# A start-up with x's first tile loaded in two halves and its third tile multiplied within contraction step 1

## The chip, the cores and the metric

The kernel runs on one core of a Trainium2 chip. The metric is the device time of one execution in microseconds (us). Four runs of the kernel before the change took 177.17 to 177.66 us, with a median of 177.25. The core has five engines that matter here: PE (matrix multiply; PEld is its weight load), DVE (vector), ACT (scalar), POOL (GpSimd) and SP (issues most DMAs). ACT can issue DMAs as well.

## What is computed

```python
xn = layernorm(x)                      # x: (2048 tokens, 512), bf16
out = x + SSM(xn) + (gelu(xn @ w_gate) * (xn @ w_up)) @ w_down

def SSM(x):                            # 512 complex states
    dt = exp(log_dt); Lam = Lambda_re + 1j * Lambda_im
    Lam_bar = exp(dt * Lam)
    Bu = x @ (((Lam_bar - 1) / Lam)[:, None] * B).T
    h[t] = Lam_bar * h[t-1] + Bu[t]
    return 2 * (h @ C.T).real + x * Dskip
```

The gate and up weights are 512 x 1376 each, w_down is 1376 x 512.

## The kernel before

The 2048 tokens are cut into 16 tiles of 128 rows, and four tiles make a block; 512 tokens of a block are one matmul's moving width. The contraction over the 512 features takes four steps (k = 0 to 3) of 128. For a block, the kernel normalises x on DVE, transposes it with DMA transposes (TR), multiplies it with w_gate and w_up (GU, L842), with B (BU, L748), runs the recurrence on DVE as a scan between two rotations (CHAIN, L773 to L803), and adds everything up in PSUM (DN, L883) before the output is added to the skip term and stored (L901).

The first block is started in another way, since at its beginning neither the normalised x nor the weights are there. Its tiles are only centred (the row mean is taken off, `sub`, `cent`), transposed by PE against an identity matrix (`cent_T`, L679), and copied from PSUM to the transposed tile XC by ACT or DVE (L686, L688). `GT_k` (L700) then multiplies one tile j by one 128-row step k of the weights, into the PSUM banks 2j and 2j + 1; the division by the standard deviation follows later, as the scale of the gelu (`GT_evac`, L720 and L723). `GT_mm` (L711) does the same for all four steps at once, for tile 3 and for further columns. So PE can start on a weight step as soon as that step has landed.

What sets the order: PE and SP run in program order. On DVE, ACT and POOL a list scheduler sets it, from modelled durations and due times; `order_behind` and `ch(...)` chain some operations by hand, and in the start-up nearly all of DVE's are. The scheduler derives all waits from which buffers overlap.

The names of the start-up: `ld_x0` (L492) loads a tile of x; tiles 0, 2 and 3 go over SP's queue, in front of and between the weight loads (`ld_wk`, L482, for gate and up of each step), tile 1 over ACT's queue, behind the instruction that loads the activation table and after DVE's second memset. Three small parameter loads (L506) follow on ACT's queue. PE begins with seven matmuls on constants (`nwarm`, L925 to L934) and with short ones in between (`fill`). Tile 0's row sum is taken on DVE (L965), tile 1's mean on ACT (L954); both tiles are centred in two pieces, of 128 and 384 columns (`cent`, L957). Tiles 2 and 3 get their mean from the layer norm's statistics on DVE (`stats`, L610 and L611; `sub`, L948). `ks(k, j, ...)` issues the step-k matmuls of tile j. In PE's order tiles 0 and 1 take steps 0 and 1, tile 2 is transposed, tiles 0 and 1 take step 2, and tile 2 then takes steps 0, 1 and 2; step 3 follows for all three, with the transposes of tile 3 behind the first of them.

Of the kernel before, what the change touches and what calls it, by code (L numbers as in the profile page):

```python
# [353 lines left out]
def d_dve_1x(n): return 100.0 + 1.04 * n  # L354
def d_dve_scan(n): return 90.0 + 2.08 * n
def d_dve_ts4x(n): return 220.0 + 0.26 * n
D_TINY = 160.0
def d_act(n, ptr=0): return 190.0 + 0.833 * n + 90.0 * ptr
# [3 lines left out]
def build(nc, ins, out):  # L362
    with ExitStack() as es:
        E = es.enter_context
        S = Sched(nc, es)
# [6 lines left out]
        def ring(parent, name, n):  # L372
            return [A.sub(parent, "%s%d" % (name, i), i) for i in range(n)]
# [14 lines left out]
        X = ring(X_all, "X", NT)  # L388
# [70 lines left out]
        x2 = ins["A_x"][0]  # L459
# [6 lines left out]
        GATE = {"before_gelu": [], "nh": 0}  # L466
        SCR = A.alloc("SCR", [1], F32)
        half = V(lambda e: e.memset(HALF.ap, 0.5), D_TINY, [], [HALF], "half")
        wrm = S.order_behind(V(lambda e: e.memset(WRM.ap, 0.0), 150, [], [WRM], "wrm"), half)
# [21 lines left out]

        def ld_x0(j, queue="sync", after=()):  # L492
            return S.dma(lambda e, j=j: e.dma_start(X[j].ap, x2[128 * j:128 * (j + 1), :]), 128 * 1024, writes=[X[j]], tag="ld_x0", queue=queue, after=after)  # L493
        ld_x0(0)
        GATE["par"] = S.order_behind(ld_x0(1, "scalar", [wrm]), GATE["table"])
        for k in range(KD):
            if k in (1, 3):
                ld_x0((k + 3) // 2)
# [109 lines left out]
        def stats(b, j):  # L608
            tt = 4 * b + j
            return (V(lambda e: e.bn_stats(ST[tt].ap, X[tt].ap), d_dve_1x(512), [X[tt]], [ST[tt]], "bnst"),  # L610
                    V(lambda e: e.bn_aggr(MVt[b][j].ap, ST[tt].ap), D_TINY, [ST[tt]], [MVt[b][j]], "bnag"))  # L611

        def root(b, j0, j1):
            mn, sbq, qb, rq = (cols(t, b, j0, j1) for t in (MN, SBQ, QB, RQ))
            mv = Buf("MV%d_%d_%d" % (b, j0, j1), "sb", MVt[b][j0].lo, MVt[b][j1 - 1].hi, MV[b].ap[:, j0:j1])
            op = V(lambda e: e.tensor_scalar(sbq.ap, mv.ap[:, :, 1], EPS_BF16, None, ALU.add), D_TINY, [mv], [sbq], "sbq")
            GATE["pow"] = POOL(lambda e: e.tensor_tensor(qb.ap, sbq.ap, HALF.ap[:, 0:j1 - j0], ALU.pow), 1100, [sbq, HALF], [qb], "pow")
            POOL(lambda e: e.tensor_copy(mn.ap, mv.ap[:, :, 0]), 200, [mv], [mn], "mn")
            return op, mn, qb, rq
# [53 lines left out]
        def cent_T(j, k0, k1, bank, eng="A", c0=0):  # L673
            pt = PS[bank].bitcast(BF16)[:, c0:c0 + 128 * (k1 - k0)]

            def f(e):
                ins_ = None
                for k in range(k0, k1):
                    ins_ = e.transpose(pt[:, 128 * (k - k0):128 * (k - k0 + 1)], XN[j].ap[:, 128 * k:128 * (k + 1)], IDN.ap)  # L679
                return ins_  # L680
            PE(f, 56.0 * (k1 - k0), [XNp[j][k0 > 0] if j < 2 else XN[j], IDN], [BANK[bank]], "T0")
            dst, src = XC_all.ap[:, k0:k1, 128 * j:128 * (j + 1)], pt.rearrange("p (q t) -> p q t", t=128)
            w = XCs[j] if k1 - k0 == KD else [XCs[j][k0 > 0]]
            sc = 1.0 if j else 1.0 / D
            if eng == "A":
                GATE["evTA"] = ACT(lambda e: e.activation(dst, src, ACTF.Copy, scale=sc), d_act(128 * (k1 - k0)), [BANK[bank]], w, "evT")  # L686
                return GATE["evTA"]
            return V(lambda e: e.tensor_scalar(dst, src, sc, None, ALU.mult), 110 + 0.6 * 128 * (k1 - k0), [BANK[bank]], w, "evT")  # L688
# [3 lines left out]
        def acc(j, u):  # L692
            return 2 * j + u

        def GT_k(k, j, u, ws, first=False):
            f0, f1 = FR[u]
            w = f1 - f0
            bank = acc(j, u)
            dst = PS[bank][:, w * ws[0]:w * (ws[-1] + 1)].rearrange("p (w f) -> p w f", w=len(ws))
            PE(lambda e: e.matmul(dst, XCd(j, k), WGU[:, ws[0]:ws[-1] + 1, k, f0:f1], start=first, stop=k == KD - 1, skip_group_check=True),  # L700
               d_pe([w * len(ws)]), [(WGc, WUc)[w_][k] for w_ in ws] + [XCs[j][k > 0]] + ([] if first else [BANK[bank]]), [BANK[bank]], "GK")

        def GT_mm(j, u, bank):
            f0, f1 = FR[u]
            w = f1 - f0
            dst = PS[bank][:, 0:2 * w].rearrange("p (w f) -> p w f", w=2)

            def f(e):
                ins_ = None
                for k in range(KD):  # L710
                    ins_ = e.matmul(dst, XCd(j, k), WGU[:, :, k, f0:f1], start=(k == 0), stop=(k == KD - 1))  # L711
                return ins_
            PE(f, d_pe([2 * w] * KD), wdeps(WGc, 2 * u) + wdeps(WUc, 2 * u) + XCs[j], [BANK[bank]], "GT")

        def GT_evac(j, u, bank):
            f0, f1 = FR[u]
            w = f1 - f0
            GATE["nh"] = kk = (GATE["nh"] + 1) % 3
            sc, rb = rss[j]
            GATE["last_gelu"] = ACT(lambda e: e.activation(GG[kk].ap[:, 0:w], PS[bank][:, 0:w], ACTF.Gelu_apprx_tanh, scale=sc),  # L720
                                    d_act(w, 1), [BANK[bank], rb], [GG[kk]], "gelu")
            hp = Buf("H0_%d_%d" % (j, u), "sb", H0[j].lo + 2 * f0, H0[j].lo + 2 * f1)
            V(lambda e: e.scalar_tensor_tensor(H0[j].ap[:, f0:f1], PS[bank][:, w:2 * w], sc, GG[kk].ap[:, 0:w], ALU.mult, ALU.mult),  # L723
              d_dve_1x(w), [BANK[bank], GG[kk], rb], [hp], "hmul")
# [7 lines left out]
        def TR(b, js=range(4)):  # L732
            for j in js:
                tt = 4 * b + j
                S.dma(lambda e, b=b, j=j, tt=tt: e.dma_start_transpose(
                    XNT[b].ap[:, :, 128 * j:128 * (j + 1)], XN[tt % 8].ap),
                    1.6 * 128 * 1024, reads=[XN[tt % 8]], writes=[XTk[b][j]], tag="tr_x%d" % b, issue=1280.0)
# [184 lines left out]
                for j in range(4):  # L922
                    seed(j); hidden(j); states(j); store(j)

        nwarm = 7  # L925
        ones, ones4 = nc.const_aps.tensor(1.0, (128, 128), BF16), nc.const_aps.tensor(1.0, (128, 512), BF16)
        wb = 4

# [16 lines left out]
        def ch(*ops):  # L945
            for op in ops:
                tail_op[0] = S.order_behind(op, tail_op[0])
        def sub(j):  # L948
            return V(lambda e: e.tensor_scalar(XN[j].ap, X[j].ap, MVt[0][j].ap[:, 0:1], None, ALU.subtract),
                     d_dve_ts4x(512), [X[j], MVt[0][j]], [XN[j]], "sub")  # L950
# [20 lines left out]
        def ks(k, j, w_, first=False):  # L971
            for u in range(2):
                GT_k(k, j, u, w_, first)
# [4 lines left out]
        ks(0, 1, [0], True)  # L978
        cent_T(1, 1, 4, 5)
        ks(0, 1, [1])  # L980
        for j in range(2):
            ks(1, j, [0, 1])
        ch(*stats(0, 2)); ch(sub(2)); ch(*stats(0, 0)); ch(*stats(0, 1))
        op, mn0, qb0, rq0 = root(0, 0, 3)
        ch(op)
        ch(*stats(0, 3)); ch(sub(3))
# [5 lines left out]
            ch(norms(0, [j], mn0, rq0, 0))  # L992
        ch(recip(qb3, rq3))
        TR(0, [0, 1])
        cent_T(2, 0, 4, 7)
        for j in range(2):
            ks(2, j, [0, 1])
        for k in range(3):
            ks(k, 2, [0, 1], k == 0)
        for j in range(3):  # L1000
            ks(3, j, [0, 1])
            for u in range(2):
                GT_evac(j, u, acc(j, u))
            if j == 0:
                cent_T(3, 0, 4, 6)
        for (j, u), bank in zip([(3, 0), (3, 1), (0, 2), (0, 3), (1, 2), (1, 3), (2, 2), (2, 3), (3, 2), (3, 3)],
                                (7, 6, 0, 1, 2, 3, 4, 5, 0, 7)):
            GT_mm(j, u, bank)
            GT_evac(j, u, bank)
        rstate["n"] = 2  # L1010
# [41 lines left out]
def bass_parallel_sum__ssm_conv_s5__geglu_ffn__prompt_kernel(  # L1052
    nc: bass.Bass,
    A_x: bass.AP,
    A_Lambda_re: bass.AP,
    A_Lambda_im: bass.AP,
    A_B_re: bass.AP,
    A_B_im: bass.AP,
    A_C_re: bass.AP,
    A_C_im: bass.AP,  # L1060
    A_log_dt: bass.AP,
    A_Dskip: bass.AP,
    B_x: bass.AP,
    B_w_gate: bass.AP,
    B_w_up: bass.AP,
    B_w_down: bass.AP,
    out: bass.AP,
):
    ins = {
        "A_x": A_x, "A_Lambda_re": A_Lambda_re, "A_Lambda_im": A_Lambda_im,  # L1070
        "A_B_re": A_B_re, "A_B_im": A_B_im, "A_C_re": A_C_re, "A_C_im": A_C_im,
        "A_log_dt": A_log_dt, "A_Dskip": A_Dskip,
        "B_w_gate": B_w_gate, "B_w_up": B_w_up, "B_w_down": B_w_down,
    }
    build(nc, ins, out)
# [28 lines left out]
```

## Time and profile before

| | us |
|---|---|
| median of four runs | 177.25 |
| the profiled execution, its own time | 177.15 |
| its span in the profile | 175.8 |
| PE busy | 172.0 |
| DVE busy | 159.7 |
| ACT busy | 95.5 |
| POOL busy | 10.8 |

The start-up by stretches of the span, as busy time of the engines (us) and the rate of the DMA engines:

| stretch, us | length | PE | DVE | ACT | GB/s |
|---|---|---|---|---|---|
| 0.7 to 4.0 | 3.30 | 3.23 | 2.43 | 2.21 | 187 |
| 4.0 to 7.6 | 3.60 | 3.19 | 3.21 | 1.45 | 258 |
| 7.6 to 11.4 | 3.80 | 3.80 | 3.06 | 1.57 | 292 |
| 11.4 to 18.4 | 7.00 | 6.96 | 6.00 | 5.27 | 216 |

Busy time is the time in which at least one instruction of the engine is under way. For PE it includes the constant matmuls of the lead-in, and the drain of the last matmul of a run, so that a short wait can be hidden in it. The starts of the rows tell more than their lengths. A wait in the profile is time in which the engine had nothing under way, put down to what ended it.

### The profile page before, as it was taken

Reading aid. Unit: us, or ns where it says so; the run is one execution under the profiler, and the core shown is the slowest. Engines: PE = TensorE matmul, PEld = TensorE weight load, DVE = VectorE, ACT = ScalarE, POOL = GpSimd, SP = SyncE. Lnnn points to the kernel's source line nnn. Section 1 sums busy time; section 2 is a strip of 40 time slices with the busy share of each in tenths; the row PEclk is TensorE's granted clock in tenths of the full one; section 3 lists DMA queues with packets and bytes.
Section 4 is the critical chain, followed back from the end, with each engine's and each line's share of the span. In section 5 each row is a group of like instructions: output and inputs, shape, how many; then the busy total and the mean of one; then the engine's idle time right before and its main releaser. Section 6 shows DMA issues by size and latency. Waiting matters only on the chain.

```text
span 175.8 us, 2494 instructions
## 1 busy us (share of the span) xinstructions
PE 172.0 (98%) x868; PEld 83.8 (48%) x883; DVE 159.7 (91%) x279; ACT 95.5 (54%) x185; POOL 10.8 (6%) x24
## 2 busy tenths in 40 slices
PE   8999999999999999999999999999999999999995
PEld 3545564644544444444644444444464444444454
DVE  6987999986999989889899999989999899999941
ACT  5467577899876899383676792000667970000000
POOL 3122030202000000002200000000000000000000
DMA  5899989695899000002015000002001000000321
GB/s 165 248 338 144 257 166 197 118 131 112 159 304 245 2 4 2 0 30 78 15 34 113 4 0 0 4 0 89 30 0 30 4 0 0 0 0 0 118 67 60
DMA packets 32420, 14.36 MB, mean 82 GB/s; under 512 B 23736, under 2 KB 32408, under 8 KB 32408
## 3 DMA queue, kind: packets, MB, share of 16 engines
q1 hardware_dynamic: 32240, 14.07, 36.2%
q8 instruction: 7, 0.11, 0.2%
q10 hardware_dynamic: 168, 0.13, 0.2%
q14 instruction: 5, 0.04, 0.1%
HBM read 6.46 MB, written 2.10 MB: 49 GB/s over the span
## 4 chain that ended last, share of the span: by engine, by line
PE 94%; DMA 2%; SPq 2%; issue 1%; DVE 0%
PE PS L883 37%; PE PS L842 32%; PE PS L748 16%; PE PS L711 4%; PE PS L816 3%; PE PS L700 2%; DMA arena<-in_B_w_up_dram 2%; SPq L484 1%; SPq L493 0%; DVE arena L901 0%; PE PS L679 0%
## 5 line engine op out<-in xcount | busy, mean ns | idle before, releaser
L883 PE MATMUL PS<-arena 128*128 128x512 bf16 (+3 forms) x317 | 65.9, 366 | 0.3
L842 PE MATMUL PS<-arena 128*128 128x512 bf16 x257 | 57.1, 379 | 0.4
L883 PEld LDWEIGHTS PS<-arena 128*128 128x128 bf16 (+1 forms) x323 | 30.8, 98 | 35.2
L842 PEld LDWEIGHTS PS<-arena 128*128 128x128 bf16 x264 | 25.8, 98 | 30.2
L786 DVE TENSOR_TENSOR_SCAN arena<-arena 128x512 bf16<-128x512 f32 x32 | 38.9, 1254 | 0.0
L857 ACT ACTIVATE arena<-PS 128x512 bf16<-128x512 f32 x33 | 19.8, 599 | 25.9 <-DVE arena L901 16.7
L748 PE MATMUL PS<-arena 128*128 128x512 bf16 (+1 forms) x134 | 28.0, 366 | 0.1
L861 ACT ACTIVATE arena<-PS 128x512 bf16<-128x512 f32 x33 | 19.8, 599 | 5.1 <-PE PS L842 5.1
L875 ACT ACTIVATE PS<-arena 128x512 f32<-128x512 bf16 (+2 forms) x17 | 9.6, 581 | 19.7 <-DVE arena L901 19.0
L748 PEld LDWEIGHTS PS<-arena 128*128 128x128 bf16 x136 | 13.3, 98 | 14.1
L757 ACT ACTIVATE arena<-PS 128x512 bf16<-128x512 f32 x32 | 17.7, 593 | 2.3 <-PE PS L748 2.3
L901 DVE TENSOR_TENSOR arena<-PS,arena 128x512 bf16<-128x512 f32 (+2 forms) x17 | 10.9, 653 | 6.4 <-PE PS L883 5.5
L863 DVE TENSOR_TENSOR arena<-arena 128x512 bf16<-128x512 bf16 x33 | 13.1, 414 | 1.7 <-ACT arena L861 1.6
L775 DVE TENSOR_TENSOR arena<-arena 128x4096 bf16<-128x4096 bf16 (+1 forms) x5 | 9.2, 1859 | 0.8 <-ACT arena L606 0.8
L773 DVE TENSOR_TENSOR arena<-arena 128x4096 bf16<-128x4096 bf16 (+1 forms) x5 | 9.2, 1860 | 0.3 <-ACT arena L605 0.3
L798 DVE TENSOR_TENSOR arena<-arena 128x4096 bf16<-128x4096 bf16 x4 | 9.2, 2288 | 0.1
L799 DVE TENSOR_TENSOR arena<-arena 128x4096 bf16<-128x4096 bf16 x4 | 9.1, 2284 | 0.0
L720 ACT ACTIVATE arena<-PS,arena 128x256 bf16<-128x256 f32 (+1 forms) x16 | 6.5, 448 | 4.0 <-PE PS L700 2.2
L610 DVE BATCH_NORM_STATS2 arena<-arena 128x6 f32<-128x512 bf16 x12 | 7.7, 679 | 0.2 <-DMA arena<-in_A_x_dram 0.2
L711 PE MATMUL PS<-arena 128*128 128x512 bf16 (+1 forms) x40 | 7.1, 336 | 0.0
L723 DVE SCALAR_TENSOR_TENSOR arena<-PS,arena 128x256 bf16<-128x256 f32 (+1 forms) x16 | 6.3, 444 | 0.5 <-PE PS L700 0.5
L700 PE MATMUL PS<-arena 128*128 128x512 bf16 (+1 forms) x28 | 6.2, 349 | 0.4 <-DMA arena<-in_B_w_up_dram 0.2
(96 smaller groups left out, 124.4 us busy)
## 6 DMA issues: line engine op xcount, KB each, us to landing
out_dram<-arena SPq DMA_DIRECT2D x15, 128.0 KB, 1.7
arena<-in_A_x_dram SPq DMA_DIRECT2D x3, 512.0 KB, 5.4
arena<-in_B_w_down_dram SPq DMA_DIRECT2D x1, 1280.0 KB, 8.4
arena<-in_B_w_gate_dram SPq DMA_DIRECT2D x4, 128.0 KB, 2.9
arena<-in_B_w_up_dram SPq DMA_DIRECT2D x4, 128.0 KB, 3.2
arena<-in_B_w_gate_dram SPq DMA_DIRECT2D x1, 480.0 KB, 6.4
arena<-in_B_w_up_dram SPq DMA_DIRECT2D x1, 480.0 KB, 7.3
arena<-arena SPq DMA_TRANSPOSE x25, 3.0
```

The costliest lines, as they stand in the source:

```text
L700: PE(lambda e: e.matmul(dst, XCd(j, k), WGU[:, ws[0]:ws[-1] + 1, k, f0:f1], start=first, stop=k == KD - 1, skip_group_check=True), d_pe([w ...
L711: ins_ = e.matmul(dst, XCd(j, k), WGU[:, :, k, f0:f1], start=(k == 0), stop=(k == KD - 1))
L748: ins_ = e.matmul(PS[bank][:, 128 * j0:128 * j1], BBT[c][dk].ap[:, 128 * s:128 * (s + 1)], XNT[b].ap[:, dk, 128 * j0:128 * j1], start=(dk ...
L757: GATE["evBu"] = ACT(lambda e, bank=bank, k3=k3, s=s, c=c: e.activation(SSc[k3][s][c].ap, PS[bank][:, :], ACTF.Copy), d_act(512), [BANK[ba ...
L786: V(lambda e, g=g, rb=rb, init=init: e.tensor_tensor_scan(g.ap, rb, g.ap, init, ALU.mult, ALU.add), d_dve_scan(512), [g, PA[RRr]] + ([CARc ...
L842: ins_ = e.matmul(PS[bank][0:m, c0:c1], W.ap[:, dk, 128 * ft:128 * ft + m], XNT[b].ap[:, dk, c0:c1], start=(dk == 0), stop=(dk == KD - 1))
L857: GATE["last_gelu"] = ACT(lambda e, bg=bg, kk=kk, m=m: e.activation(GG[kk].ap[0:m, :], PS[bg][0:m, :], ACTF.Gelu_apprx_tanh), d_act(512), ...
L861: ACT(lambda e, bu=bu, kk=kk, m=m: e.activation(UPB[kk].ap[0:m, :], PS[bu][0:m, :], ACTF.Copy), d_act(512), [BANK[bu]], [UPB[kk]], "evU")
L863: V(lambda e, kk=kk, m=m, ft=ft, k2=k2: e.tensor_tensor(HTt[k2][ft].ap[0:m, :], GG[kk].ap[0:m, :], UPB[kk].ap[0:m, :], ALU.mult), d_dve_tt ...
L875: ACT(lambda e: e.activation(PS[bank][:, c0:c1], X[tt].ap[:, c0:c1], ACTF.Copy), d_act(c1 - c0), [X[tt]], [BANK[bank]], "seed")
L883: ins_ = e.matmul(PS[bank][:, c0:c1], l_[:, 128 * j:128 * (j + 1)], r_[:, c0:c1], start=False, stop=last and n == len(ops) - 1, skip_group ...
L901: V(lambda e: e.tensor_tensor(OUTB[ko].ap[:, c0:c1], PS[bank][:, c0:c1], XD[tt].ap[:, c0:c1], ALU.add), d_dve_1x(c1 - c0), [BANK[bank], XD ...
```

## The change

Tile 0 of x is loaded as two halves of 64 rows, one over SP's queue and one over ACT's, where it stands ahead of tile 1; neither ACT load waits for DVE's memset any longer. One of the seven constant matmuls is left out. Tile 2's transposes are put behind the step-1 matmuls of tile 0, in two pieces (step 0 alone, steps 1 to 3), with an eviction for each; its matmuls of steps 0 and 1 stand ahead of step 2. Tile 3's transposes and the first `GT_mm` swap the banks 6 and 7.

```diff
-        ld_x0(0)
-        GATE["par"] = S.order_behind(ld_x0(1, "scalar", [wrm]), GATE["table"])
+        X0p = [Buf("X0p%d" % i, "sb", X[0].lo, X[0].hi) for i in range(2)]
+
+        def ld_x0p(i, queue):
+            q0, q1 = 64 * i, 64 * (i + 1)
+            return S.dma(lambda e: e.dma_start(X[0].ap[q0:q1, :], x2[q0:q1, :]), 64 * 1024, writes=[X0p[i]], tag="ld_x0", queue=queue, issue=300.0)
+        x0a, x0b = ld_x0p(0, "sync"), ld_x0p(1, "scalar")
+        x0b.deps.remove(x0a)
+        x0a.users.remove(x0b)
+        S.order_behind(x0b, GATE["table"])
+        GATE["par"] = S.order_behind(ld_x0(1, "scalar"), x0b)
...
-        nwarm = 7
+        nwarm = 6
...
         ks(0, 1, [1])
-        for j in range(2):
-            ks(1, j, [0, 1])
-        ch(*stats(0, 2)); ch(sub(2)); ch(*stats(0, 0)); ch(*stats(0, 1))
+        ch(*stats(0, 2)); ch(sub(2))
+        ks(1, 0, [0, 1])
+        cent_T(2, 0, 1, 7)
+        cent_T(2, 1, 4, 6)
+        ks(1, 1, [0, 1])
+        ks(0, 2, [0, 1], True)
+        ch(*stats(0, 0)); ch(*stats(0, 1))
...
         TR(0, [0, 1])
-        cent_T(2, 0, 4, 7)
-        for j in range(2):
+        ks(1, 2, [0, 1])
+        for j in range(3):
             ks(2, j, [0, 1])
-        for k in range(3):
-            ks(k, 2, [0, 1], k == 0)
         for j in range(3):
             ks(3, j, [0, 1])
             for u in range(2):
                 GT_evac(j, u, acc(j, u))
             if j == 0:
-                cent_T(3, 0, 4, 6)
+                cent_T(3, 0, 4, 7)
         for (j, u), bank in zip([(3, 0), (3, 1), (0, 2), (0, 3), (1, 2), (1, 3), (2, 2), (2, 3), (3, 2), (3, 3)],
-                                (7, 6, 0, 1, 2, 3, 4, 5, 0, 7)):
+                                (6, 7, 0, 1, 2, 3, 4, 5, 0, 7)):
             GT_mm(j, u, bank)
             GT_evac(j, u, bank)
```

## The prediction

> **What bounds the kernel now.** I read the page's busy table first: PE is busy for 172.0 of 175.8 us. Then the chain of waits in order of time, to see where the chain is anything else than PE:
>
> ```profile
> 4.03 3.42 DMA arena<-in_B_w_up_dram
> 7.46 0.14 issue
> 7.59 2.75 PE PS L700 x12
> 10.34 0.22 PE PS L679 x4
> 10.57 0.86 PE PS L700 x4
> 11.43 6.93 PE PS L711 x40
> ```
>
> Columns: start, length (us), what, number of instructions. Up to 7.46 the chain is DMA: SP's row of weight issues, then the landing of w_up of contraction step 2. From 7.59 on it is PE alone, with gaps of 0.05, down to the last output add at 174.03. So a matmul taken out after 7.59 shortens the kernel by its length, and only waits before 7.59 can be removed. The last rows also give prices: 0.86 for four 512-column matmuls is 0.216 each, 0.22 for four transposes is 0.056 each.
>
> Next the timeline of PE alone, for what it did before 7.59:
>
> ```profile
> 5.62 0.33 PE L679 MATMUL PS<-arena 128*128 128x128 bf16 x3
> 5.79 1.35 PE L700 MATMUL PS<-arena 128*128 128x256 bf16 x6
> 6.98 0.39 PE L679 MATMUL PS<-arena 128*128 128x128 bf16 x4
> 7.59 0.38 PE L700 MATMUL PS<-arena 128*128 128x512 bf16 x1 [0.23 <-DMA arena<-in_B_w_up_dram]
> ```
>
> The row at 6.98 holds tile 2's four transposes. They occupy 4 x 0.056, so PE is free at 7.20 (a row's 0.39 includes the drain of the last one), and the next matmul starts at 7.59. The hole is 0.39 us, not the 0.23 in the bracket.
>
> Last, what tile 2 has to wait for, on DVE and ACT:
>
> ```profile
> 5.02 0.70 DVE L610 BATCH_NORM_STATS2 arena<-arena 128x6 f32<-128x512 bf16 x1 [0.18 <-DMA arena<-in_A_x_dram]
> ...
> 5.97 0.35 DVE L949 TENSOR_SCALAR arena<-arena 128x512 bf16<-128x512 bf16 x1
> ...
> 5.07 1.42 ACT L686 ACTIVATE arena<-PS 128x128 bf16<-128x128 bf16 x3 [1.09 <-PE PS L679]
> 7.41 0.60 ACT L686 ACTIVATE arena<-PS 128x512 bf16<-128x512 bf16 x1 [0.92 <-PE PS L679]
> ```
>
> Tile 2 lands at 5.0 and is centred by 6.32; DVE is the gate of its transposes. ACT has three evictions from 5.07 to 6.49 and then nothing until 7.41, so there is room for tile 2's.
>
> **What the Trainium skill says.** "DMA: Bandwidth & Descriptors", section "Rules for kernel authors", advises against splitting a transfer into partition halves: both spray over the same 16 engines. Before shows x tiles 0 and 1 on two queues together, each 2.2 us to landing; whether a half lands sooner it doesn't show. "Perfetto Trace Analysis", section "DVE / Act Engine Instruction", has such an instruction wait in a queue while its sequencer goes on. The trace agrees: the x load issues from ACT's queue at 0.99, the ACTIVATE ahead of it runs at 2.02. "TensorE: Matmul & The Clock Gate", Part 1, puts PE at half rate until about 3.4 us of sustained activity. The trace agrees in rate: the lead-in's weight loads at 1.15, 1.58, 2.01, 2.43 and 2.86 are 0.43 apart for 512 columns, and the four fill matmuls from 4.02 take 0.39 together, which is 0.056 apart plus the drain. The rate rises between 3.71 and 4.02.
>
> **The change, part by part.**
>
> *Halves of x.* SP's first issue (0.40) covers 64 rows; I leave SP's later issues where they are, at most 0.1 earlier. ACT's queue now issues half of x first, without the wait for DVE's second memset that held x tile 1 until 0.99, so near 0.76; x tile 1 follows near 1.15, some 0.15 later than before, and the three parameter loads behind it slip as much (they landed by 4.2, and their reader on SP is issued at 8.15). Gain on x tile 0, which the sum on DVE awaits until 2.92: between 0 (the engines are shared) and 0.3 (half the packets per queue); I take 0.15. Tile 1 would land near 3.4 instead of 3.23; its mean (0.63 + 0.19) ends near 4.15, where DVE came to it at 4.36. So the opening moves forward by 0.15, or not at all. What is late next is x tile 2, at 5.0, whose issue at 2.13 hardly moves. Worth to the end: 0 to 0.1.
>
> *One warm-up matmul less.* It frees PE 0.43 earlier (3.29 instead of 3.71), where it then waits for DVE's centring (transpose at 3.96, perhaps 3.8). Worth nothing in itself; its risk is rival C.
>
> *Tile 2 within step 1.* Nothing is taken out of PE's work; the same matmuls fill the hole. Slots, from the row at 5.79: two of 256 columns and the two of step 1 of tile 0 end at 5.79 + 0.22 + 0.43 = 6.44; the kernel of before loses some 0.07 here to an ACT eviction, so 6.51. Centring of tile 2 ends at 6.32, plus 0.09 to reach PE (as from 3.86 to the load at 3.95): 6.41, in time. Transposes 6.51 to 6.74; step 1 of tile 1 to 7.17; step 0 of tile 2 to 7.60; step 1 of tile 2 to 8.03. ACT must keep up: the first eviction (128 columns, 0.28) starts at 6.51 + 0.22 drain + 0.04 = 6.77 and ends at 7.05, needed at 7.17; the second (384 columns, 0.49) ends at 7.54, needed at 7.60. Two evictions cost ACT 0.77 instead of 0.60; ACT is idle there. The margin of the second is 0.06 only.
>
> Then step 2, needed at 8.03 and landed at 7.46: the DMA is off the path. Six matmuls to 9.33, then step 3. Its w_up is issued at 5.46 and takes 3.6 to landing by the DMA view, 9.03 to 9.06: in time by 0.3. Step 3 of tile 0 to 9.76; tile 3's transposes need its centring, which ends at 9.34 in DVE's unchanged hand order. Transposes to 9.98; four matmuls to 10.84, where the first L711 starts. It starts at 11.27 before (10.40 + 4 x 0.216). Gain: 11.27 - 10.84 = 0.43, which is the 0.39 hole plus two gaps of 0.02.
>
> *Further on.* The second weight chunk (step-wise GT of columns 512 up) is issued at 6.41 and lands 5.5 later, at 11.9; its first reader moves from 13.0 to 12.57. The transposes of the normalised x go out from SP between 10.49 and 15.67, bound by SP; the last lands near 16.9, the first GU matmul needs it at 18.41, then 17.98. B_re lands at 23.0 for 24.4. The first output states, at 73.7, need C's last scaling on DVE at 71.8. The last recurrence is done at 161.7, its reader comes near 164.6. All margins exceed 0.43, so it should reach the end. On DVE nothing is moved in fact: the statistics and centring of tile 2, written earlier in the program now, stood first in the hand-written chain before too, and the sum on DVE gains one semaphore wait (two loads instead of one), some 0.06. Only what isn't chained by hand may be set in another order by the planner, which works from modelled times; with PE never waiting after 7.59 that can only lose, and it is counted in B. The swapped banks 6 and 7 wait for evictions that are long past.
>
> Sum: 0.43, plus 0 to 0.1 from the opening, minus 0 to 0.1 for the narrow eviction: 0.4. The profiled execution took 177.15 (span 175.8 and 1.35 around it) and becomes 176.75; the median of the runs shown is 177.25, 0.10 above the profiled one, so 176.8.
>
> **Rivals.**
>
> *B: the hole only moves.* If tile 2's second eviction is late (ACT serving something else), or the eviction of tile 3, now at 10.2 beside the first gelu, is queued behind a second gelu (0.47 less some 0.1 of cover), or step 3's weights slip past 9.33 because the halves reorder the engines' packets, PE waits there instead. For: margins of 0.06 and 0.3. Against: each is a margin, none is negative, and before had the order gelu, eviction, gelu with no PE wait. Time: 177.0 to 177.3. The same comes out if the step doesn't do what it says.
>
> *C: the clock comes late, the slower side.* The lead-in of before keeps PE busy from 0.77 to about 3.8 almost without a break, and the rate rises between 3.71 and 4.02. With one matmul less PE is idle from 3.4 to 3.8. If the activity over a window of 3.4 us falls under what raises the rate, PE stays at half rate for another window, to about 7.3. The work from the first transpose to the second of step 1's pairs is then: up to 7.3 about 4,100 columns at 0.83 ns instead of 0.42; laid out slot by slot with DVE's and ACT's waits, step 1 of tile 0 ends near 7.56 instead of 6.51, 1.05 late. Less the gain of 0.43 this is +0.6: 177.85. It decides from a delay of 0.43 on. For: the lead-in is exactly what is cut. Against: fill and transposes follow soon, four runs lie within 0.5, and no view shows the threshold.
>
> **How the numbers follow.** A (gain of 0.3 to 0.55) 0.60; B 0.20; C 0.20. 0.2% (0.35 us) is about what a measurement of this kernel can tell from no change. A is centred at 0.4, with its thin lower edge, 0.03, under 0.35; B is within; C is slower. Faster 0.57, same 0.23, slower 0.20. The time is A's, 176.8. The low end is A's best, 176.55 (0.43 plus 0.1, plus the spread of runs); the high end takes in B and half of C, 177.8, leaving out some 0.1 above and 0.04 below. A alone: 176.55 to 177.0.
>
> **What would show it.** In the chain the long DMA piece ends before PE's long run begins, and the run starts at PE's first matmul behind x tile 2, near 6.5, without a hole to 10.84. The first L711 starts at 10.8 to 10.9. In the PE timeline no gap above 0.1 stands between 6.5 and 10.8. DVE's sum begins near 2.75. C would show as weight loads 0.43 apart, or transposes 0.11 apart, beyond 4.1. The forecast is wrong if the first L711 starts at 11.2 or later, or if it starts early and a wait above 0.1 stands on PE after it.

## The result and the profile after

The changed kernel took 178.76 us, median of 44 runs (177.39 to 180.53); before took 177.31 in 63 runs beside them. Over the runs that compare, the ratio is 1.0069, with a 95% interval of 1.0055 to 1.0083: slower, where faster was forecast. The times fall into groups: 16 of the 44 lie at 177.4 to 178.0, 28 at 178.4 or above, most of these near 179.4. The profiled execution (179.28, span 178.0) is of the upper group.

The chain of waits of the changed kernel, start-up only (start, length, what; pieces under 0.1 us are left out):

```profile
0.74 0.70 ACT L470
1.48 3.23 DMA arena<-in_A_x_dram
4.73 0.73 ACT arena L962 x2
5.56 0.27 DVE arena L970
5.87 0.29 PE PS L687
...
7.65 1.28 PE PS L708 x4
8.93 0.43 PE PS L687 x4
9.36 3.10 PE PS L708 x14
12.46 0.22 PE PS L687 x4
12.68 0.86 PE PS L708 x4
```

Before, the chain ran through SP's weight issues to w_up of step 2. Now it runs through x tile 1: issued at 1.48 on ACT's queue, landed 3.23 us later at 4.71 (3.23 before), its mean at 5.46, its centring, its first transpose at 5.87. From 9.36 the prices are the old ones (four matmuls in 0.86, four transposes in 0.22). Ahead of it they are double: four matmuls of half or full width in 1.28, four transposes in 0.43.

PE's timeline shows both losses:

```profile
3.29 0.31 PE L947 MATMUL PS<-const-bfloat16-1.0 128*128 128x128 bf16 x1
4.36 0.29 PE L687 MATMUL PS<-arena 128*128 128x128 bf16 x1 [0.76 <-DVE arena L968]
4.44 0.63 PE L947 MATMUL PS<-const-bfloat16-1.0 128*128 128x128 bf16 x4
5.06 0.58 PE L708 MATMUL PS<-arena 128*128 128x256 bf16 x2
5.87 0.29 PE L687 MATMUL PS<-arena 128*128 128x128 bf16 x1 [0.23 <-DVE arena L970]
...
9.15 3.31 PE L708 MATMUL PS<-arena 128*128 128x512 bf16 x14
12.30 0.39 PE L687 MATMUL PS<-arena 128*128 128x128 bf16 x4
...
13.38 1.89 PE L719 MATMUL PS<-arena 128*128 128x512 bf16 x8
```

PE stands still from about 3.4 to 4.36, then waits again for tile 1. The fill row at 4.44 (0.63 for four, before 0.39 at 4.02) shows the half rate; it lasts until 9.36, where the chain's prices change. But the hole ahead of step 2 is gone, as forecast: tile 2's transposes and then fourteen matmuls run without a gap. The first GT matmul (L719, before L711) starts at 13.38 instead of 11.27. That is 2.11 later, and the profiled time is 179.28 - 177.15 = 2.13 longer: all of the loss lies ahead of this point.

ACT and its queue in the same execution:

```profile
0.91 0.53 ACTq L498 DMA_DIRECT2D arena<-in_A_x_dram  x1
1.48 0.74 ACTq L493 DMA_DIRECT2D arena<-in_A_x_dram  x1
...
4.73 0.63 ACT L962 ACTIVATE arena<-arena 128x512 bf16<-128x512 bf16 x1 [2.49 <-DMA arena<-in_A_x_dram]
```

The load of 64 rows takes 0.53 to issue, longer than the one of 128 rows did before (0.38). The one behind it takes 0.74. The first bytes move later too. The stretch from 1.7 to 2.0, first in the kernel before and then in the changed one (busy time of PE, PEld, DVE, ACT and POOL, the clock, and last the share of the DMA engines and GB/s):

```profile
1.70:2.00 0.30, 0.30 (x2) 0.03 (x1) 0.30 (x1) 0.30 (x1) 0.30 (x3) 1.00 0.93 137
1.70:2.00 0.30, 0.30 (x2) 0.03 (x1) 0.30 (x1) 0.30 (x1) 0.30 (x3) 1.00 0.00 0
```

Before, data flow from 1.7 on; in the changed kernel nothing moves before 2.1. The clock column reads 1.00 where PE runs at half rate too, so the rate is read from the lengths of PE's rows.

### The profile page after: what moved, and what is told of

Its sections match the earlier page's. It is cut to its first block, busy times and chain, and to the rows that moved or that the text cites. A ratio compares the mean times of both kernels' runs of the same rounds, so it can differ in the third digit from the quotient of the medians.

```text
span 178.0 us, 2495 instructions
## 1 busy us (share of the span) xinstructions
PE 173.6 (98%) x867; PEld 84.9 (48%) x882; DVE 159.8 (90%) x279; ACT 95.7 (54%) x186; POOL 10.7 (6%) x24
## 4 chain that ended last, share of the span: by engine, by line
PE 95%; DMA 2%; ACT 1%; issue 1%; DVE 0%; DVEq 0%
PE PS L891 37%; PE PS L850 32%; PE PS L756 15%; PE PS L719 4%; PE PS L708 3%; PE PS L824 3%; DMA arena<-in_A_x_dram 2%; PE PS L687 1%; ACT arena L962 0%; ACT L470 0%; DVE arena L909 0%; DVE arena L970 0%; DVEq L337 0%
## 5 line engine op out<-in xcount | busy, mean ns | idle before, releaser
L756 PE MATMUL PS<-arena 128*128 128x512 bf16 (+1 forms) x134 | 28.0, 366 | 0.1
L708 PE MATMUL PS<-arena 128*128 128x512 bf16 (+1 forms) x28 | 7.7, 412 | 0.0
L719 PE MATMUL PS<-arena 128*128 128x512 bf16 (+1 forms) x40 | 7.1, 336 | 0.0
```

What stands on the lines that cost most here:

```text
L756: ins_ = e.matmul(PS[bank][:, 128 * j0:128 * j1], BBT[c][dk].ap[:, 128 * s:128 * (s + 1)], XNT[b].ap[:, dk, 128 * j0:128 * j1], start=(dk ...
```

## The experiments

Times of kernels are medians, beside runs of the kernel before on the same chip. "First GT" is the start of the first L711 matmul (whatever its line in that kernel) in the kernel's profile. Three dots in a diff or a view stand for lines left out; the last row of a view of PE can be cut short by the end of the stretch asked for.

**The parts one at a time.** The first kernel has only the new order of PE's matmuls:

```diff
 (against the changed kernel)
+        ld_x0(0)
+        GATE["par"] = S.order_behind(ld_x0(1, "scalar", [wrm]), GATE["table"])
...
-        x0a, x0b = ld_x0p(0, "sync"), ld_x0p(1, "scalar")
...
-        nwarm = 6
+        nwarm = 7
```

> Only the new order of PE's matmuls (tile 2 within step 1), with one whole load of x tile 0 and seven constant matmuls. If the order is sound and the loss comes from the other two parts: the hole of 0.39 us before step 2 is gone, the first L711 starts near 10.85 and the median is about 0.4 us below before (176.9). If the order itself loses (tile 2's eviction late, or another order set by the planner): 177.3 or more, with a wait above 0.1 us on PE between 6.5 and 11.

Measured: 177.28 (14 runs), ratio 0.9995, interval 0.9984 to 1.0007. No loss, and no measurable gain. Its profiled execution (176.88) does show the mechanism:

```profile
4.13 0.51 PE L939 MATMUL PS<-const-bfloat16-1.0 128*128 128x128 bf16 x4
...
5.95 0.89 PE L700 MATMUL PS<-arena 128*128 128x256 bf16 x4
6.67 0.39 PE L679 MATMUL PS<-arena 128*128 128x128 bf16 x4
6.89 3.19 PE L700 MATMUL PS<-arena 128*128 128x512 bf16 x14
...
11.00 2.32 PE L711 MATMUL PS<-arena 128*128 128x512 bf16 x10
```

No hole, and the first GT at 11.00: 0.27 earlier than before, and the time is 0.27 shorter than before's profiled 177.15. Here the rate rises within the fill row at 4.13 (0.51, between the 0.39 and the 0.63 seen elsewhere). So the gain exists in an execution; why it isn't in the median is taken up below.

The second kernel has only the two half loads, with before's order and seven constant matmuls:

```diff
 (against the kernel before)
-        ld_x0(0)
-        GATE["par"] = S.order_behind(ld_x0(1, "scalar", [wrm]), GATE["table"])
...
+        x0a, x0b = ld_x0p(0, "sync"), ld_x0p(1, "scalar")
+        x0b.deps.remove(x0a)
+        x0a.users.remove(x0b)
+        S.order_behind(x0b, GATE["table"])
+        GATE["par"] = S.order_behind(ld_x0(1, "scalar"), x0b)
```

> Only the two half loads of x tile 0, with before's order and seven constant matmuls. Load theory: two queues issuing at once make each issue about 0.55 instead of 0.4 us, tile 0 is ready at 3.2 to 3.3 instead of 2.9, tile 1 at 4.3 to 4.7 instead of 3.2, and tile 2 near 5.8; PE's steps 0 and 1 run 0.7 to 1.0 us later, of which the hole hides 0.4: 0.3 to 0.6 us slower (177.6 to 177.9). Clock theory alone (only the lead-in matters): 177.3, unchanged.

Measured: 177.80 (21 runs), ratio 1.0044, interval 1.0025 to 1.0062. Fifteen runs lie at 177.5 to 178.0, six above 178.4. The load theory holds with its size; a clock that only the lead-in sets doesn't explain it. Its profiled execution (178.45) has the first GT at 11.68, only 0.41 late, and then another wait that no other profile here has:

```profile
11.68 7.09 PE L719 MATMUL PS<-arena 128*128 128x512 bf16 x40
19.46 5.34 PE L850 MATMUL PS<-arena 128*128 128x512 bf16 x24 [0.69 <-DMA arena<-arena]
```

The last transpose of the first block's x, issued at 15.15, landed 4.18 us later; in the kernel before it took 2.5. This is one execution; that it comes from the halves is not shown.

The third kernel has only one constant matmul less:

```diff
-        nwarm = 7
+        nwarm = 6
```

> Only one constant matmul less, before's loads and order. Clock theory: in some executions PE's full rate comes one window later, so the times fall into two groups, one near 177.3 and one 0.5 to 1.2 us above; the median rises by 0.1 to 0.6 us. Load theory alone: no difference, 177.3, since PE only waits in the time that it frees.

Measured: 177.42 (14 runs, 177.08 to 177.77), ratio 1.0006, interval 0.9995 to 1.0016. No upper group, and no difference that can be told. So the cut alone does no harm that these runs can tell, and the clock theory's two groups did not come. Its profile (177.49) shows why it might have: the rate rises only within the row at 6.30, and before's order still comes off cheaply.

```profile
6.30 0.38 PE L679 MATMUL PS<-arena 128*128 128x128 bf16 x3
6.51 1.35 PE L700 MATMUL PS<-arena 128*128 128x256 bf16 x6
7.70 0.39 PE L679 MATMUL PS<-arena 128*128 128x128 bf16 x4
7.92 2.75 PE L700 MATMUL PS<-arena 128*128 128x512 bf16 x12
```

Tile 2's transposes are 0.72 later than before (7.70 against 6.98), step 2 only 0.33 (7.92 against 7.59): the hole is used up. The first GT is at 11.60, the time 0.34 longer.

The fourth is the changed kernel with seven constant matmuls again (`nwarm = 7` in place of 6).

> The changed kernel with seven constant matmuls again. Clock theory: fewer executions with the late rate, median 177.4 to 177.9 instead of 178.8. Load theory alone: PE is as late as in the changed kernel, 178.5 or more.

Measured: 177.78 (22 runs), ratio 1.0034, interval 1.0019 to 1.0049. Nineteen runs lie at 177.4 to 178.2, three near 179.4. As the clock theory expects, the seventh matmul takes most of the upper group away (3 of 22 runs at 178.3 or above instead of 28 of 44; the two sets were not taken side by side). The rest of the loss stays. The profiled execution fell in the upper group (179.36) and has the rate rise above 9 again, first GT at 13.43.

**Is PE's idle time what delays the rate?** Two kernels fill it in the changed kernel with short constant matmuls, the second kernel at both gaps:

```diff
 (first kernel)
-        fill(1)
+        fill(9)
 (second kernel, in addition)
         ks(0, 0, [0], True)
+        fill(4)
```

> The changed kernel with nine short constant matmuls instead of one ahead of the first transpose, and nothing else: PE's idle time from 3.4 to 4.36 is filled. Clock theory: the slower group near 179.3 is gone or rare, median 177.6 to 178.2. If the idle time isn't what delays the rate: the slower group stays with about half of the executions, median 178.5 or more.

> The changed kernel with PE's gaps filled: nine instead of one short constant matmul ahead of the first transpose, and four more behind the first step-0 pair; six long ones as in the changed kernel. Clock theory: PE is active nearly without a break from 0.77, the late rise of the rate (above 9 us) and with it the slower group of times (near 179.3) is gone, median near 177.7. If the slower group has another cause (loads, planner): it stays, median 178.3 or more.

Measured: the first 177.82 (11 runs: ten at 177.34 to 178.09, one at 179.75); the second 178.27 (6 runs, 178.01 to 178.55). At 179 and above lie 1 of these 17 runs and 19 of the 44 of the changed kernel. So filling the idle time ahead of the first transpose takes nearly all of that group away.

The length of this idle time alone doesn't decide it. With only six constant matmuls PE stands still from 3.39 to 3.94, and none of 14 runs lies above 177.77. With the halves by columns (below) it stands still only from 3.82 to 4.12, and 6 of 18 lie at 179.3 or above; there PE waits a second time, for tile 1, ahead of 5.63. Every kernel with tile 0 in halves and this gap unfilled has runs at 179 or above (19 of 44 of the changed kernel, 5 of 21 with only the halves, 3 of 22 with seven constant matmuls, 3 of 4 and 6 of 18 in the two kernels of the last part), and no kernel that loads it whole has one.

The second kernel's median missed its expectation (near 177.7) and comes close to the 178.3 that stood for another cause. Its chain shows that the four added fill matmuls had become work on the path, still at half rate:

```profile
5.02 0.57 PE PS L708 x2
5.59 0.43 PE PS L947 x4
6.01 0.11 PE PS L687
```

**A second profile of each.** The two kernels of the comparison were profiled once more, unchanged.

> The changed kernel once more, for a second profile. Clock theory: if the execution falls in the faster group (177.4 to 178.0), PE's rate rises before 7 and the first L719 starts near 11.5 to 12; if it falls in the slower group (179.3), the rate rises above 9 again and the first L719 starts near 13.3. Load theory alone: the first L719 starts at the same point in both, 13 or later.

> The kernel before once more, for a second profile. Clock theory: the point where PE's rate rises differs from the first profile's (3.7 to 4.0) by up to 2 to 3 us, yet the first L711 starts at 11.3 to 11.6, since the hole ahead of step 2 takes most of it up. If the rise is tied to the program's start: it lies between 3.7 and 4.1 again.

The changed kernel took 177.50 this time. PE's timeline:

```profile
4.29 0.23 PE L687 MATMUL PS<-arena 128*128 128x128 bf16 x1 [0.69 <-DVE arena L968]
4.35 0.39 PE L947 MATMUL PS<-const-bfloat16-1.0 128*128 128x128 bf16 x4
...
5.50 0.23 PE L687 MATMUL PS<-arena 128*128 128x128 bf16 x1 [0.20 <-DVE arena L970]
...
11.60 0.59 PE L719 MATMUL PS<-arena 128*128 128x512 bf16 x2
```

The loads are late here too (first transpose at 4.29), though tile 1 landed at 4.34 instead of 4.71, so that its first transpose is at 5.50 instead of 5.87. The rate is the full one from the first transpose on. The first GT is at 11.60, 1.78 earlier than in the first profile, and the time is 1.78 shorter. Of this, 0.37 is tile 1's earlier landing. From its first transpose to the first GT it is 7.51 in the first profile and 6.10 in this one, so the late rate costs about 1.4, in one and the same kernel. The profile of the kernel with `fill(9)`, whose full rate comes before tile 1's transpose at 5.82 and whose first GT is at 11.86, agrees with 6.04. What is left against before, 0.33 at the first GT and 0.35 in the time, is what the late loads cost after all that the new order gives back; how it divides is not shown.

The kernel before took 177.15 again:

```profile
4.02 0.63 PE L939 MATMUL PS<-const-bfloat16-1.0 128*128 128x128 bf16 x4
4.64 0.38 PE L700 MATMUL PS<-arena 128*128 128x256 bf16 x2
...
7.03 0.39 PE L679 MATMUL PS<-arena 128*128 128x128 bf16 x4
7.58 2.75 PE L700 MATMUL PS<-arena 128*128 128x512 bf16 x12 [0.17 <-DMA arena<-in_B_w_up_dram]
```

Here the rate rises between 4.4 and 4.7, later than in the first profile, yet step 2 starts at 7.58 and the first GT at 11.26, as before. So the rise isn't tied to the program's start. Its delay comes to only 0.05 at tile 2's transposes (7.03 against 6.98), and the hole takes that up.

**Does the new order gain anything?** The first kernel was run once more.

> The kernel with only the new order once more, for its times and a second profile. Clock theory: where PE's rate rises before 4.3, the first L711 starts near 10.9 to 11.0; where it rises later, it starts later by about half of the delay, as no hole is left to take it up; the times spread more than before's, and the median stays within 0.2 us of before. If the order gains what was forecast and the first fourteen times were chance: median 176.9.

Measured: 177.22 (21 runs) beside 177.38 for before, ratio 0.9991, interval 0.9981 to 1.0000. Its profiled execution (177.22):

```profile
4.06 0.63 PE L939 MATMUL PS<-const-bfloat16-1.0 128*128 128x128 bf16 x4
...
6.13 1.03 PE L700 MATMUL PS<-arena 128*128 128x256 bf16 x4
...
11.33 1.03 PE L711 MATMUL PS<-arena 128*128 128x512 bf16 x4
```

The fill row takes the full 0.63, the rate rises between 5.2 and 5.6, and the first GT is at 11.33. The row with the last 256-column matmuls and step 1 of tile 0 starts at 5.79 in the first profile of before, and at 5.95 and 6.13 in the two profiles of the new order. From there to the first GT it is 5.48 before (5.42 in its second profile), and 5.05 and 5.20 with the new order. So the step itself gives 0.43 in one profile, just as forecast, and 0.28 in the other. But PE reaches it 0.16 and 0.34 later, and with no hole left this lateness goes through to the end. What remains of the gain is 0.27 and -0.06.

The times do not spread more than before's, against the expectation; the median within 0.2 us of before is as expected. The intervals of both sets of runs allow a gain of 0 to 0.28 us, less than the 0.43 of the forecast.

A variant loads x tile 2 from ACT's queue, so that SP is free for the weights earlier:

```diff
 (against the kernel with only the new order)
-            if k in (1, 3):
-                ld_x0((k + 3) // 2)
+            if k == 1:
+                GATE["par"] = S.order_behind(ld_x0(2, "scalar"), GATE["par"])
+            if k == 3:
+                ld_x0(3)
```

> Only the new order, one whole load of tile 0, seven constant matmuls, and x tile 2 issued from ACT's queue behind tile 1 (near 1.4 instead of 2.13), so that SP issues every weight from step 1 on 0.47 earlier. If DMA issue still bounds the start-up beside the clock: tile 2 near 4.2, step 2 near 7.2, first L711 at 10.7 or earlier, median 176.7 to 177.0. If the clock's rise alone sets what the new order gives: 177.2 to 177.3.

Measured: 177.28 (14 runs), ratio 0.9998, interval 0.9987 to 1.0009. No gain. The tile was issued at 1.44 but took 3.4 us to landing, so it was there at 4.84 and not at 4.2; the profile's first GT is at 11.24 with the rate rising near 5.3.

**What makes the half loads dear?** First, both halves on SP, tile 1 on ACT's queue as before, with before's order and seven constant matmuls:

```diff
 (against the kernel with only the halves)
-        x0a, x0b = ld_x0p(0, "sync"), ld_x0p(1, "scalar")
+        x0a, x0b = ld_x0p(0, "sync"), ld_x0p(1, "sync")
...
-        S.order_behind(x0b, GATE["table"])
-        GATE["par"] = S.order_behind(ld_x0(1, "scalar"), x0b)
+        GATE["par"] = S.order_behind(ld_x0(1, "scalar", [wrm]), GATE["table"])
```

> Before's order and lead-in, x tile 0 as two halves that are both issued by SP, tile 1 on ACT's queue at 0.99 as before. Collision theory (two queues issuing at once stretch each other): each half is issued in 0.3 to 0.4 us, tile 1 lands near 3.3, weights slip by one issue of 0.4: 177.4 to 177.6. If a load of 64 rows is dear in itself: each half takes 0.55 or more on SP too, weights slip by 0.7, 177.7 or more.

Measured: 179.24 (4 runs, 178.27 to 179.48), ratio 1.0094, interval 1.0070 to 1.0119. SP's and ACT's issues:

```profile
0.73 1.21 SPq L498 DMA_DIRECT2D arena<-in_A_x_dram  x2
1.99 0.59 SPq L484 DMA_DIRECT2D arena<-in_B_w_gate_dram  x1
...
0.99 0.39 ACTq L493 DMA_DIRECT2D arena<-in_A_x_dram  x1
1.43 0.76 ACTq L513 DMA_DIRECT2D arena<-in_A_log_dt_dram  x1
```

Each half takes 0.57 to 0.58 on SP (1.21 for both with the step between them), while ACT's 128-row load beside them takes 0.39 as ever. SP's whole load before, with the same ACT load beside it, took 0.40. So it isn't two queues in each other's way: the 64-row load is dear in itself. The issue that overlaps or follows the halves is stretched too (0.59 instead of 0.41, 0.76 instead of 0.57).

Second, the halves by columns, so that each load has 128 rows of 512 bytes:

```diff
 (against the kernel with only the halves; the second pair is a piece of its line)
-            q0, q1 = 64 * i, 64 * (i + 1)
+            q0, q1 = 256 * i, 256 * (i + 1)
-e.dma_start(X[0].ap[q0:q1, :], x2[q0:q1, :])
+e.dma_start(X[0].ap[:, q0:q1], x2[0:128, q0:q1])
```

> Before's order and lead-in, x tile 0 in two halves by columns (128 rows of 512 bytes each) over the two queues, instead of halves by rows. If a load of 64 rows is what makes the issue dear: each half is issued in about 0.4, tile 1 near 1.4, landing at 3.5 to 3.7, median 177.3 to 177.5. If any second load ahead of tile 1 costs the same: 177.8, as with the halves by rows.

Measured: 177.69 (18 runs, six of them at 179.3 and above), ratio 1.0048, interval 1.0024 to 1.0072. The issues are cheap, as expected, and it doesn't help:

```profile
0.91 0.39 ACTq L498 DMA_DIRECT2D arena<-in_A_x_dram  x1
1.34 0.45 ACTq L493 DMA_DIRECT2D arena<-in_A_x_dram  x1
```

Tile 1, issued at 1.34, took 3.1 us to landing and came at 4.5, not at 3.5 to 3.7. The tile 2 of the variant above, second on ACT's queue in the same way, took 3.4. Tile 1 before took 2.2: it was issued at 0.99, ahead of SP's first weight load at 1.21. So cheap issues alone buy nothing: tile 1 comes at 4.5 here and at 4.3 to 4.7 with the halves by rows. That it waits behind the weight load fits all of these times, but no run moved its place alone.

The place isn't all of it either. With both halves on SP, tile 1 was issued at 0.99 as before and ahead of every weight load, and still took 2.7, landing at 3.7. There the late start of all transfers shows: in the seven profiles with halves by rows no byte moves before 2.0, in the seven others, the halves by columns among them, the first moves between 1.7 and 1.8. Why a load of 64 rows has this effect is not shown.

## Why the prediction was wrong

- *Halves of x.* This is the first step that failed. It put the gain on tile 0 between 0 and 0.3, and tile 1 at 3.4. In the first profile tile 0's halves landed near 3.0 and 3.2 instead of the whole near 2.9, and DVE's sum starts at 3.33 instead of 2.92. Tile 1 landed at 4.71 in one profile and 4.34 in the other. Three terms were mis-sized. The issue of 64 rows was taken as no longer than that of 128 (0.40); it is 0.53 to 0.58, and the first bytes move 0.3 to 0.4 later. ACT's issues were put at 0.76 and 1.15; they are at 0.91 and 1.48. And tile 1, now behind a weight load, kept its 2.2 to landing; it is 2.85 to 3.23. The price is 0.53 us in the median with before's order (177.80 against 177.27). The wait for a second load, put at 0.06, is of the right order: DVE's sum starts 0.10 behind the later half (3.27 behind 3.17, with only the halves).
- The prediction cited the Trainium skill's "DMA: Bandwidth & Descriptors", section "Rules for kernel authors", against halves of partitions, and then took 0.15 of gain. The runs agree with the page's advice: DVE's sum, which needs all of tile 0, starts at 2.91 to 3.02 in the six profiles with one whole load, at 3.08 with the halves by columns, and at 3.25 or later in the seven profiles with halves by rows.
- *One warm-up matmul less.* "Worth nothing in itself" is right alone (177.42, interval across 1), and wrong beside the late loads: 28 of 44 runs in the upper group with six, 3 of 22 with seven. The prediction priced the part on its own, with the first transpose at 3.8 to 3.96; it came at 4.36.
- *Rival C* named the mechanism and undersized it: idle from 3.4 to 3.8, half rate to about 7.3, +0.6. With the late loads PE is idle to 4.36, the half rate can last to 9.36, and it then costs about 1.4; tile 1's landing adds to it. It also had a chance of 0.20 only, since the two parts were priced apart: the one that was to bring the first transpose forward pushed it back into C's ground.
- *Tile 2 within step 1.* The mechanism is right: no hole, tile 2's second eviction not late, step 3's weights in time. Counted from the matmuls at 5.79 the size is right in one profile (0.43) and 0.28 in the other. The step failed in its starting point: it took the 5.79 of one profile as fixed, and the new order starts at 5.95 and 6.13. What reaches the first GT is 0.27 and -0.06, in the medians 0 to 0.16. The hole had been a buffer for a late start, which is not the same in each execution; without it the lateness goes through. A small misreading changes nothing: the way from DVE to PE was taken as 0.09, but tile 0's first centring ends at 3.89 (0.25 from 3.64) and PE's load starts at 3.95.
- *Further on.* Right where the profiles show it: the shift of the first GT equals that of the time within 0.03 in both profiles of the changed kernel and in those with only the new order. Two kernels differ by more than 0.1: the one with only the halves, for its late transpose (0.41 at the first GT, 1.30 in the time), and the one with both gaps filled (0.71 and 0.95), where the rest isn't explained.

How much PE must be active, over what stretch, for its rate to rise is not shown by these runs; they show that filling the gap works, not which of the gaps counts. The runs between 178.3 and 178.9 were not profiled in the changed kernel, so their cause stays open. No version clearly beat the kernel before; the new order alone is as fast or up to 0.28 us faster.

## What to carry to other kernels

Before a load is split or moved, write down the order of all issues of all queues, since what slips behind a large load can pay for it at landing (tile 1 here: 2.2 us before, 2.85 to 3.23 behind a weight load). In the first microseconds, a late input can cost PE twice, as it did here, once as a wait and once as a clock that stays slow, so parts that touch the opening are priced together and not one by one. And a hole just ahead of a wait may be the buffer that keeps an uncertain start from showing; look at a second profile before counting it as a gain.

## What the runs showed of the hardware

- A load of 64 rows of 1 KB took 0.53 to 0.58 us to issue, one of 128 rows of 1 KB 0.38 to 0.46, one of 128 rows of 512 bytes 0.39 to 0.40. Fewer rows were not cheaper. A load of 128 rows issued right behind one of 64 took 0.56 to 0.74.
- With a first load of 64 rows no data moved before 2.0 (seven profiles); with one of 128 rows, of 1 KB or of 512 bytes, the first moved between 1.7 and 1.8 (seven profiles).
- The rise of PE's rate came at 3.7 to 4.0 and at 4.4 to 4.7 in two executions of the kernel before. In the changed kernel, with PE idle from 3.4 to about 4.3 in both, it came above 9 in one execution and by 4.29 in the other. With seven constant matmuls and PE idle from 3.8 to 4.31 it came above 9 too. The Trainium skill's "TensorE: Matmul & The Clock Gate", Part 1, says of the activity window that it is free-running and doesn't reset when a kernel starts; the two profiles of the kernel before agree.
- The same DMA transpose landed 4.18 us after its issue in one execution of the kernel with only the halves and 2.5 in the profile of the kernel before.
